# Decode attention block: wide Q chunks, paired PV matmuls, single score banks and a software pipeline one stage deeper

## The chip, the cores and the metric

The kernel runs on one core of one Trainium2 chip. The metric is the time of one execution on the device in microseconds (us); lower is better. The kernel before stands at 206.03 us, the median of 4 runs (204.81 to 207.11). Engines are named as in the profile: PE (matmul), PEld (weight load), DVE (vector), ACT (scalar), POOL, SP (issues DMAs).

## The reference, cut to what matters

A transformer block for one decode token and a batch of 2. Per batch and head (32 heads of 192), one query row meets the last 1024 rows of a K and a V cache; then come an output projection and a gated FFN. Layer norms are modulated by a projected condition `c`.

```python
mod = silu(c) @ w_mod                                  # 640 x 3840 weights
h = layernorm(x) * (1 + ca) + sa
q = (h @ wq).reshape(2, 1, 32, 192)                    # 640 x 6144
scores = einsum('bhqd,bhkd->bhqk', q, k[:, :, -1024:]) * 192 ** -0.5
o = einsum('bhqk,bhkd->bhqd', softmax(scores), v[:, :, -1024:])
x = x + ga * (o @ wo)                                  # 6144 x 640
h = layernorm(x) * (1 + cb) + sb
x = x + gb * ((gelu(h @ w_gate) * (h @ w_up)) @ w_down)
```

Every weight and every cache row is read once: 76.88 MB, all bf16.

## The kernel before

All large loads go through the SP queue in one order: the first third of `w_mod`, four parts of `wq`, the rest of `w_mod`, 64 cache items of 768 KB (K or V of one head, both batches) through a ring of 10 slots, then `wo`, `w_gate`, `w_up`, `w_down`. A "group" is two heads times two batches: four units, two K items and two V items. Scores are made on DVE and PE: DVE multiplies K by the broadcast query (`mul`), PE adds up 32-column chunks of the product in PSUM with identity matmuls (`red`), and DVE sums the last 32 columns (`D3`). Then comes the softmax chain: maximum over partitions by a transpose (`T`), its broadcast (`Bc`), `D7`, `exp`, then `PV`.

```python
BK_S = (0, 1, 2, 3)                       # score banks: two for even groups, two for odd
declare_q(QL - 1)                         # QL = NG: all 32 Q units, here, ahead of attention
mod_part(1)
...
for g in range(NG + 1):
    d_mul(g, 0); p_reduce(g, 0)
    chain_a1(g - 1)                       # D3 over 128x1024 f32, D4, T
    filler(g)                             # nothing left to do: QL = NG and ND = 0
    d_mul(g, 1); declare_ring([4 * g]); p_reduce(g, 1)
    chain_a2(g - 1)                       # D5, D6 (ACT), Bc (PE)
    d_mul(g, 2); p_reduce(g, 2)
    chain_a3(g - 1)                       # D7, exp (ACT)
    p_pv(g - 1)                           # 32 matmuls of 192 columns
    declare_ring([4 * (g - 1) + 2, 4 * (g - 1) + 3])   # V slots free: next loads
    filler(g)
    d_mul(g, 3); declare_ring([4 * g + 1]); p_reduce(g, 3)
    chain_b1(g - 1); chain_b2(g - 1)      # divide, select rows, transpose into oT
# (guards for the first and last g are cut)
```

Each engine runs its list in order; a scheduler puts in the semaphore waits from declared reads and writes.

## Time and profile before

| | before |
|---|---|
| span of the profiled run | 203.3 us |
| PE, DVE busy | 68%, 46% |
| load stream (queue 1) | 99.1% of 16 engines' time |
| first attention multiply | 45.6 us |
| a group when nothing makes it wait | 6.36 us |
| a group of loads (4 x 768 KB) | 7.8 us |

The page of the kernel before; the row of 40 slices is mean DMA busy share in tenths, below it GB/s; a group line has count, busy us, mean ns and idle time with its releaser; the last line gives KB and the median time from issue to landing.

```profile
PE 139.0 (68%) x1809; PEld 93.2 (46%) x1809; DVE 92.7 (46%) x176; ACT 45.8 (23%) x140; POOL 1.2 (1%) x9
...
DMA  5999999999999999999999999999999999999990
GB/s 171 407 402 401 401 413 411 400 401 401 401 342 413 399 399 400 401 402 399 402 402 401 399 402 399 403 400 401 402 400 403 386 363 363 362 369 398 394 332 28
...
q1 hardware_dynamic: 30468, 76.88, 99.1%
...
L423 PE MATMUL ps<-prod,ident_b 128*128 128x256 bf16 x384 | 63.1, 312 | 19.3 <-DVE prod L410 19.2
L410 DVE TENSOR_TENSOR prod<-ring,qbc 128x1536 bf16<-128x1536 bf16 x64 | 60.4, 948 | 8.8 <-DMA ring<-in_A_k_cache_dram 8.4
...
L370 PE MATMUL ps<-r 128*128 128x384 bf16 x160 | 27.7, 338 | 3.3 <-DVE r L351 3.3
...
L471 DVE TENSOR_REDUCE S_sb<-ps 128x32 f32<-128x1024 f32 x16 | 19.5, 1218 | 1.5 <-PE ps L423 1.5
...
ring<-in_A_k_cache_dram SPq DMA_DIRECT2D x32, 768.0 KB, 9.7
```

The load stream is the bottleneck: 9 in every slice but the first and last, and the multiplies (L410) idle for K loads. The stretch of 363 GB/s at slices 32 to 35 is `wo`, whose rows are 1280 B, as are those of `w_down` at the very end; everything else has rows of 2560 B and more and runs at about 400.

The chain of waits through one group at the one place where compute doesn't wait for loads (start us, us, what):

```profile
57.34 0.96 DVE prod L410
58.29 1.15 DVE S_sb L471
...
59.46 0.19 DVE M L475
59.65 0.88 DVE prod L410
...
60.57 0.83 PE ps L423 x6
61.40 0.31 PE ps L486 x2
61.71 0.76 PE ps L423 x6
62.47 0.76 PE ps L437 x31
...
63.32 0.28 ACT junk L448 x2
...
63.70 0.96 DVE prod L410
```

From multiply to multiply 6.36 us: this is what a group costs when its data is there. Loads need 7.8 us for the same group, so compute catches up with the loads and then waits for them.

One hole in the stream, by stretches of half a us (columns: busy time of PE, PEld, DVE, ACT, POOL, then PE clock, DMA share, GB/s):

```profile
58.00:58.50 0.50, 0.49 (x6) 0.37 (x7) 0.50 (x2) 0.12 (x1) 0.00 (x0) 1.00 0.81 184
58.50:59.00 0.50, 0.50 (x6) 0.36 (x4) 0.50 (x1) 0.05 (x1) 0.00 (x0) 1.00 0.79 160
```

The 32 Q units and the `mod` matmuls hold the first multiply back to 45.6 us, so no V slot comes free before 57 us and the stream dips.

### The profile page before, as it was taken

The numbers are of one execution on the slowest core, as the hardware profiler recorded it, in microseconds if no ns is written. First come the engines' busy times: TensorE is split into PE (matmuls) and PEld (weight loads), VectorE is DVE, ScalarE is ACT, GpSimd is POOL, SyncE is SP. The second block draws the span as 40 slices with busy tenths as digits, with TensorE's granted clock in tenths as the row PEclk, the third lists the DMA queues.
The fourth block names the chain that finished last, engine by engine and source line by source line (L and its number), as shares of the span: only waits on it lengthen the run. The fifth ranks groups of instructions, "written<-read, shape, count | busy, mean of one in ns | idle before, by whom it ended". The sixth has DMA issues, their size and how long they took to land.

```text
span 203.3 us, 4191 instructions
## 1 busy us (share of the span) xinstructions
PE 139.0 (68%) x1809; PEld 93.2 (46%) x1809; DVE 92.7 (46%) x176; ACT 45.8 (23%) x140; POOL 1.2 (1%) x9
## 2 busy tenths in 40 slices
PE   0339999978768774975976876849758766434343
PEld 0315555556445552643544544526525435434342
DVE  0050000008877786595586595675765840001300
ACT  2124566520322211111122121112112123000300
POOL 2000000000000000000000000000000000000000
PEclk9999999985999999698599699797978785555555
DMA  5999999999999999999999999999999999999990
GB/s 171 407 402 401 401 413 411 400 401 401 401 342 413 399 399 400 401 402 399 402 402 401 399 402 399 403 400 401 402 400 403 386 363 363 362 369 398 394 332 28
DMA packets 30526, 77.15 MB, mean 379 GB/s; under 512 B 1324, under 2 KB 9004, under 8 KB 30508
## 3 DMA queue, kind: packets, MB, share of 16 engines
q1 hardware_dynamic: 30468, 76.88, 99.1%
q8 instruction: 14, 0.23, 0.5%
q14 instruction: 4, 0.03, 0.0%
q10 hardware_dynamic: 40, 0.01, 0.0%
HBM read 76.88 MB, written 0.00 MB: 378 GB/s over the span
## 4 chain that ended last, share of the span: by engine, by line
PE 33%; DMA 26%; SPq 20%; DVE 16%; ACT 2%; issue 1%
SPq L247 20%; DMA ring<-in_A_k_cache_dram 17%; PE ps L370 14%; PE ps L423 10%; DVE prod L410 8%; DMA r<-in_B_w_down_dram 5%; DVE S_sb L471 5%; PE ps L437 4%; DMA r<-in_w_mod_dram 4%; PE ps L338 2%; PE ps L486 2%; DVE M L475 1%; ACT L494 1%; ACT junk L448 1%; DVE r L351 0%
## 5 line engine op out<-in xcount | busy, mean ns | idle before, releaser
L423 PE MATMUL ps<-prod,ident_b 128*128 128x256 bf16 x384 | 63.1, 312 | 19.3 <-DVE prod L410 19.2
L410 DVE TENSOR_TENSOR prod<-ring,qbc 128x1536 bf16<-128x1536 bf16 x64 | 60.4, 948 | 8.8 <-DMA ring<-in_A_k_cache_dram 8.4
L423 PEld LDWEIGHTS ps<-prod,ident_b 128*128 128x128 bf16 x384 | 36.8, 109 | 32.2 <-DVE prod L410 23.1
L370 PE MATMUL ps<-r 128*128 128x384 bf16 x160 | 27.7, 338 | 3.3 <-DVE r L351 3.3
L370 PEld LDWEIGHTS ps<-r 128*128 128x128 bf16 x160 | 15.2, 100 | 15.5 <-ACT qbc L374 3.6
L471 DVE TENSOR_REDUCE S_sb<-ps 128x32 f32<-128x1024 f32 x16 | 19.5, 1218 | 1.5 <-PE ps L423 1.5
L374 ACT ACTIVATE qbc<-ps 128x384 bf16<-128x384 f32 x32 | 15.7, 491 | 14.6 <-PE ps L370 14.6
L484 ACT ACTIVATE diag<-ident_f,gmn 4x4 f32<-4x4 f32 x16 | 4.7, 296 | 49.7 <-DVE gmn L482 49.7
L437 PE MATMUL ps<-ring,E_sb 128*1 128x192 bf16 x512 | 15.2, 267 | 0.7 <-ACT E_sb L494 0.7
L396 DVE TENSOR_SCALAR opc<-modT 128x10 f32<-128x10 f32 x1 | 0.2, 173 | 31.3 <-ACT modT L343 31.3
L437 PEld LDWEIGHTS ps<-ring,E_sb 128*1 128x1 bf16 x512 | 10.6, 89 | 5.4 <-ACT E_sb L494 3.0
L551 PE MATMUL ps<-oT,r 128*128 128x2 bf16 x240 | 7.0, 165 | 8.4 <-DMA r<-in_A_wo_dram 8.4
L450 DVE RECIPROCAL rden<-den 128x1 f32<-128x1 f32 x16 | 2.6, 164 | 19.0 <-ACT junk L448 19.0
L551 PEld LDWEIGHTS ps<-oT,r 128*128 128x128 bf16 x240 | 6.7, 104 | 8.6 <-DMA r<-in_A_wo_dram 8.6
L477 PE MATMUL ps<-ident_f,M 128*4 128x128 f32 x16 | 4.6, 290 | 8.0 <-DVE M L475 7.9
L486 PEld LDWEIGHTS ps<-diag,ones_f 4*128 4x128 f32 x32 | 5.9, 229 | 5.4 <-issue 4.5
L448 ACT ACTIVATE junk<-ps 128x8 f32<-128x8 f32 x16 | 2.8, 178 | 22.6 <-PE ps L440 22.6
L494 ACT ACTIVATE E_sb<-Sb_sb 128x32 bf16<-128x32 f32 x16 | 3.7, 229 | 18.9 <-DVE Sb_sb L491 18.9
L486 PE MATMUL ps<-diag,ones_f 4*128 4x4 f32 x32 | 7.3, 296 | 0.7 <-ACT diag L484 0.7
L452 ACT ACTIVATE On<-ps,rden 128x192 bf16<-128x192 f32 x16 | 6.7, 421 | 3.9 <-DVE rden L450 3.9
L557 DVE TENSOR_TENSOR lnt<-ps,modT 128x10 f32<-128x10 f32 x1 | 0.2, 170 | 16.3 <-PE ps L551 16.3
L477 PEld LDWEIGHTS ps<-ident_f,M 128*4 128x4 f32 x16 | 1.3, 81 | 12.6 <-DVE M L475 12.6
(66 smaller groups left out, 76.8 us busy)
## 6 DMA issues: line engine op xcount, KB each, us to landing
ring<-in_A_k_cache_dram SPq DMA_DIRECT2D x32, 768.0 KB, 9.7
ring<-in_A_v_cache_dram SPq DMA_DIRECT2D x32, 768.0 KB, 12.4
r<-in_A_wq_dram SPq DMA_DIRECT2D x4, 1920.0 KB, 18.0
r<-in_A_wo_dram SPq DMA_DIRECT2D x4, 1920.0 KB, 18.7
r<-in_w_mod_dram SPq DMA_DIRECT2D x1, 3200.0 KB, 25.1
r<-in_B_w_gate_dram SPq DMA_DIRECT2D x1, 1920.0 KB, 17.4
r<-in_B_w_up_dram SPq DMA_DIRECT2D x1, 1920.0 KB, 17.0
r<-in_w_mod_dram SPq DMA_DIRECT2D x1, 1600.0 KB, 7.1
```

Of the source, the lines that this page charges most:

```text
L247: return lambda e: e.dma_start(dst, src)
L370: last = e.matmul(ps[:, bk, 0:QN], lhsT=hbc_v[:, k, b, :], rhs=wq_v[:, k, g * QN:(g + 1) * QN], start=(k == 0), stop=(k == KT - 1))
L374: S.op("act", (lambda g, b, bk: lambda e: e.activation(out=qbc[:, 2 * g:2 * g + 2, b, :], in_=ps[:, bk, 0:QN].rearrange("p (h d) -> p h d" ...
L410: return S.op("dve", lambda e: e.tensor_tensor(out=prod[:, pslot, :, :], in0=ring[:, ks, b, :, :], in1=qbc[:, h, b:b + 1, :].broadcast_to( ...
L423: last = e.matmul(o_ap, lhsT=ident_b[:, :], rhs=prod[:, pslot, :, ci * GC:(ci + 1) * GC], start=(ci == 0), stop=(ci == NCH - 1))
L437: e.matmul(ps[32 * i:32 * i + 1, BK_O, 0:Dh], lhsT=E_sb[:, z, i, j:j + 1], rhs=ring[:, vs, b, j, :], start=(j == 0), stop=(j == J - 1), ti ...
L452: S.op("act", lambda e: e.activation(out=On[:, z, :], in_=ps[:, BK_O, 0:Dh], func=ACTF.Identity, scale=rden[:, z:z + 1]), reads=[bank(BK_O ...
L471: S.op("dve", lambda e: e.tensor_reduce(out=S_sb[:, z, :, :], in_=ps[:, b0:b0 + NBG, 0:UPB * J * GC].rearrange("p k (u j c) -> p (k u) j c ...
L477: S.op("pe", lambda e: e.transpose(ps[0:4, BK_T, 0:P], M1[:, z, :], ident_f[:, :]), reads=[("M1", z), "ident_f"], writes=[bank(BK_T)], nam ...
L486: S.op("pe", lambda e: e.matmul(ps[:, BK_T, P:P + 4], lhsT=ones_f[0:4, :], rhs=diag[:, z, :], start=True, stop=True), reads=[("diag", z), ...
L494: S.op("act", lambda e: e.activation(out=E_sb[:, z, :, :], in_=Sb_sb[:, z, :, :], func=ACTF.Exp, scale=SCALE), reads=[("Sb", z)], writes=[ ...
L551: last = e.matmul(ps[:, BK_M, 2 * jn:2 * jn + 2], lhsT=wo_v[:, t, jn * P:(jn + 1) * P], rhs=oT[:, t, :], start=(t == 0 and jn == 0), stop= ...
```

## The change

Its intent, as the code shows: Q in chunks of 512 columns (24 units in place of 32 of 384), only 6 of them ahead of attention and two more per group as "filler"; after they run out, warm matmuls in the filler places to keep the PE clock up; score chunks of 64 columns (3 reduce matmuls of 512 in place of 6 of 256), which fill all four score banks with one group; PV on two key rows at a time (16 matmuls of 384 columns in place of 32 of 192); division and selection pushed one group later.

```diff
-    GC = 32
+    GC = 512 // J                        # 64: NCH = 3
-    QL = NG
-    ND = 0
+    QW = 512
+    QUP = min(2 * NQC, 2 * ((3 * 2 * Dh + QW - 1) // QW))   # 6 units ahead
+    ND = 4                               # warm matmuls per filler, 128x512
...
-        S.dma("act", ... cr ...); S.dma("act", ... xr ...)
+        S.dma("sp", ... cr ...); S.dma("sp", ... xr ...)     # ahead of w_mod
...
-            bk = BK_S[NBG * (g % 2) + i // UPB]
+            bk = BK_S[i]                 # all four banks belong to one group
...
-  in_=ps[:, b0:b0 + NBG, 0:UPB * J * GC]   # D3: 1024 elements
+  in_=ps[:, 0:4, 0:J * GC]                 # D3: 2048 elements
...
-                for j in range(J):        # PV: lhsT 128x1, rhs 128x192
+                for jp in range(J // 2):  # PV: lhsT 128x2, rhs 128x384
...
-        for g in range(NG + 1):
+        for g in range(NG + 2):
             d_mul(g, 0)
-            p_reduce(g, 0)
+            chain_b2(g - 2)
             chain_a1(g - 1)
-            filler(g)
+            p_reduce(g, 0)
+            chain_b3(g - 2)
             d_mul(g, 1); declare_ring([4 * g]); p_reduce(g, 1)
             chain_a2(g - 1)
+            filler()                      # Q unit or warm, between Bc and PV
             d_mul(g, 2); p_reduce(g, 2)
             chain_a3(g - 1); p_pv(g - 1)
             declare_ring([4 * (g - 1) + 2, 4 * (g - 1) + 3])
-            filler(g)
+            chain_b1(g - 1)
             d_mul(g, 3); declare_ring([4 * g + 1]); p_reduce(g, 3)
-            chain_b1(g - 1); chain_b2(g - 1)
+            filler()
```

(Guards, renamings and the selection matmuls of `chain_b3`, now 8 in place of 4, are cut.)

## The prediction

> **What bounds the kernel now.** The DMA engines. In the slice table the DMA row is 9 from slice 1 to 37, about 400 GB/s (363 near 162-180 us), while PE is busy 68% and DVE 46% (busy table). 76.88 MB pass in a 203.3 us span. By the landing events one K or V item (768 KB) lands every 1.95 us, so a group of four takes 7.8 us. A group's compute, where the timeline shows it not waiting for data (52 to 70 us), takes 6.4 us; later the first multiply waits for its K (idle put down to the K load, 8.4 us in all). The chain of waits ends in queued weight loads from 147 us and the last w_down landing at 200.1 us.
>
> One hole: the windows at 57.5-59.5 us show 160-330 GB/s. All 32 Q units run first (PE L370, 13.96 to 41.7 us), then the mod matmuls, so the first multiply starts at 45.65 us though its K landed about 38 us; the ring's next loads wait for PV until 57 us. That is about 0.8 us of transfer. But the landing events, 16 per load, show that the slowest DMA engine kept its 1.95 us pace through it; only leading engines idled (spread of landings fell from 1.9 to 1.2 us). The end waits for the slowest.
>
> **What the change does.**
> - Bytes, and the order of the large loads: unchanged.
> - Q: 160 matmuls of 384 become 120 of 512: same columns, but only 30 matmuls stand before attention. First multiply near 40 us. The hole goes.
> - Reduce: 384 matmuls of 256 become 192 of 512. PV: 512 of 192 become 256 of 384. Same columns, fewer instructions, little PE time.
> - D3 reads 2048 instead of 1024 elements: 1.22 us becomes about 2.3 (estimate: twice, less a fixed part). DVE per group 5.8 to 6.9 us busy, a group about 7.4: below 7.8, closer. Score banks are no longer doubled, so a group's first reduce waits for D3.
> - PV comes some 2 us later after K's landing; the ring then still has about 10 us of loads queued: no starvation. Warm matmuls: off the path.
> - The c and x loads move from the ACT queue to the head of SP. Their issues took 0.63 and 0.29 us; the w_mod load, issued at 0.81 us, and all behind it start about 0.7 us later (estimate). The Trainium skill, "DMA: Bandwidth & Descriptors", section "Issuing engines are not separate DMA queues", says a second issuing engine saves just this.
> - Instruction fetches: 14 of 16 KB in the DMA queue table, about 1.08 us each; some steps of the slowest engine's lag (0.8 to 3 us over the run) follow them. The Trainium skill, "Runtime: NRT & Kernel Launch", section "Instruction fetch mechanics", gives 256 instructions a block; 3618 PE instructions agree with 14. After: about 2900, so 11; worth about -0.5 us (estimate).
>
> **Sum.** +0.7 start, -0.5 fetches, -0.1 hole: within noise. 206.1 us, range 204.4 to 207.6. The runs before scatter from 204.8 to 207.1.
>
> **Signs.** First multiply near 40 us; no dip near 57 us; DMA share still over 97%; D3 about 2.3 us; first w_mod issue about 1.5 us; 11 fetches; last w_down landing 199.5-201; the 3.2 us tail unchanged.
>
> **What would make it wrong.** A group above 7.8 us on DVE or a cold PE (clock 0.5) for all 16 groups, draining the queue: slower by several us. Or the hole, the early multiply or fewer fetches speeding the slowest engine more than I see: at most 2-3 us.

## The result, and the profile after

| | before | after |
|---|---|---|
| median of all runs | 206.64 us (16 runs) | 212.09 us (11 runs) |
| ratio of fast runs | | 1.0259, 95% interval 1.0216 to 1.0301 |
| span of the profiled run | 203.3 us | 209.5 us |
| first attention multiply | 45.6 us | 39.6 us |
| group, start of D3 to next start of D3 | 7.8 us mostly | 8.40 us with Q units, 7.95 with warm matmuls, 9.5 twice |
| D3, mean | 1.22 us | 2.29 us |
| PE instruction fetches (16 KB) | 14 | 11 |

The ratio is the mean time of one kernel's fast runs over that of the other's of the same rounds, so it is not quite the ratio of the medians; three runs of the changed kernel over 213 us count as slow and are left out of it. The change is slower by 2.6%, although its first multiply comes 6 us earlier.

The page of the changed kernel, with the clock row as well (tenths of full PE clock granted):

```profile
PE 135.8 (65%) x1424; PEld 68.6 (33%) x1441; DVE 110.6 (53%) x176; ACT 43.6 (21%) x132; POOL 1.2 (1%) x9
...
PEclk9999965569999999999999999997998799555555
...
GB/s 128 410 399 403 403 413 409 400 402 402 400 385 372 411 356 377 388 364 409 341 358 412 312 372 381 378 404 399 360 415 353 386 370 364 363 364 396 395 339 25
...
q1 hardware_dynamic: 30508, 76.89, 97.5%
...
L396 DVE TENSOR_TENSOR prod<-ring,qbc 128x1536 bf16<-128x1536 bf16 x64 | 59.5, 947 | 6.0 <-DMA ring<-in_A_k_cache_dram 6.0
L408 PE MATMUL ps<-prod,ident_b 128*128 128x512 bf16 x192 | 54.1, 394 | 1.8 <-DVE prod L396 1.8
L415 DVE TENSOR_REDUCE S_sb<-ps 128x32 f32<-128x2048 f32 x16 | 36.7, 2291 | 3.7 <-PE ps L408 3.7
...
L373 PE MATMUL ps<-qbc,ident_b 128*128 128x512 bf16 x49 | 14.5, 418 | 0.4
...
ring<-in_A_k_cache_dram SPq DMA_DIRECT2D x32, 768.0 KB, 6.7
```

The stream is no longer steady: GB/s falls to 312 to 390 in most slices of attention, and queue 1 is busy 97.5% in place of 99.1%. The multiplies do about the same work; D3 (L415) has grown from 19.5 to 36.7 us and warm matmuls (L373) are new. K loads now land 6.7 us after issue in place of 9.7: there is less queued ahead of them. PE's clock is better than before (0.869 of full on average in the profiled run, against 0.827), so it is not what made the change slower.

The chain of waits through one group of the changed kernel:

```profile
82.65 2.30 DVE S_sb L415
...
84.98 0.20 DVE M L419
...
85.22 0.27 PE ps L421
85.49 0.65 PE ps L408 x3
...
86.46 0.67 PE ps L408 x3
87.13 0.31 PE ps L430 x2
87.44 1.20 PE ps L359 x5
...
88.66 0.60 ACT qbc L363
89.26 0.13 ACT E_sb L438
...
89.43 0.82 PE ps L450 x15
...
90.26 0.77 PE ps L408 x3
...
91.05 2.30 DVE S_sb L415
```

From D3 to D3, 8.40 us, and not one step of it is a load. The loop runs: D3 2.30, D4 0.20, transpose 0.27, first reduce 0.65, selection (in the cut lines) 0.3, second reduce 0.67, broadcast 0.31, **Q unit on PE 1.20, its eviction on ACT 0.60**, exp 0.13 (the rest of it hidden), PV 0.82, last reduce 0.77, and D3 again. Seven groups in a row have this length. With warm matmuls in the filler's place 0.97 us of them stand in the chain, and the group is 7.95 us:

```profile
121.02 0.97 PE ps L373 x4
```

Both lengths are over the 7.8 us of the loads. The wait list of the SP queue (us in total, times, longest) shows the loads waiting for PV. Before:

```profile
SPq L93 <- PE ps L440: 69.4, 13, 7.4
```

and after:

```profile
SPq L93 <- PE ps L454: 81.2, 13, 8.8
```

The landing records (16 for each load, one per DMA engine) add it up: from the last landing of the first cache item to that of the 64th, 125.0 us pass before and 131.1 us after. That is 6.1 us, about all of the difference of the two spans (6.2 us).

### The profile page after: what moved, and what is told of

It is laid out like the page before. It is cut to its first block, busy times and chain, and to the rows that moved or that the text cites. A ratio compares the mean times of both kernels' runs of the same rounds, so it can differ in the third digit from the quotient of the medians.

```text
span 209.5 us, 3411 instructions
## 1 busy us (share of the span) xinstructions
PE 135.8 (65%) x1424; PEld 68.6 (33%) x1441; DVE 110.6 (53%) x176; ACT 43.6 (21%) x132; POOL 1.2 (1%) x9
## 3 DMA queue, kind: packets, MB, share of 16 engines
q1 hardware_dynamic: 30508, 76.89, 97.5%
## 4 chain that ended last, share of the span: by engine, by line
PE 33%; SPq 32%; DVE 16%; DMA 13%; ACT 4%; issue 2%
SPq L242 32%; PE ps L408 14%; DVE S_sb L415 14%; DMA ring<-in_A_k_cache_dram 8%; DMA r<-in_B_w_down_dram 5%; PE ps L450 5%; PE ps L359 5%; PE ps L373 3%; ACT qbc L363 2%; PE ps L430 2%; PE ps L421 2%; PE ps L477 1%; DVE M L419 1%; ACT L438 1%; ACT E_sb L438 1%
## 5 line engine op out<-in xcount | busy, mean ns | idle before, releaser
L408 PE MATMUL ps<-prod,ident_b 128*128 128x512 bf16 x192 | 54.1, 394 | 1.8 <-DVE prod L396 1.8
L415 DVE TENSOR_REDUCE S_sb<-ps 128x32 f32<-128x2048 f32 x16 | 36.7, 2291 | 3.7 <-PE ps L408 3.7
L359 PE MATMUL ps<-r 128*128 128x512 bf16 x110 | 29.3, 405 | 4.3 <-DVE r L341 3.7
L363 ACT ACTIVATE qbc<-ps 128x512 bf16<-128x512 f32 x24 | 14.3, 597 | 42.4 <-PE ps L359 42.4
L408 PEld LDWEIGHTS ps<-prod,ident_b 128*128 128x128 bf16 x192 | 16.8, 100 | 18.8 <-issue 5.0
L450 PE MATMUL ps<-ring,E_sb 128*2 128x384 bf16 x256 | 13.8, 336 | 3.2 <-ACT E_sb L438 3.2
L373 PE MATMUL ps<-qbc,ident_b 128*128 128x512 bf16 x49 | 14.5, 418 | 0.4
L469 ACT ACTIVATE On<-ps,rden 128x384 bf16<-128x384 f32 x16 | 9.3, 579 | 1.8 <-DVE rden L467 1.8
L450 PEld LDWEIGHTS ps<-ring,E_sb 128*2 128x2 bf16 x256 | 4.7, 82 | 12.6 <-ACT E_sb L438 7.3
L477 PE MATMUL ps<-sel,On 128*128 128x2 bf16 (+1 forms) x64 | 7.4, 183 | 1.2 <-ACT On L469 1.2
```

The lines of the kernel that those rows point to most:

```text
L359: last = e.matmul(ps[:, bk, 0:w], lhsT=hbc_v[:, k, b, :], rhs=wq_v[:, k, c0:c0 + w], start=(k == 0), stop=(k == KT - 1))
L363: S.op("act", lambda e: e.activation(out=qbc[:, b, c0:c0 + w], in_=ps[:, bk, 0:w], func=ACTF.Copy), reads=[bank(bk)], writes=[("qbc", cq, ...
L373: last = e.matmul(ps[:, BK_Q[0], 0:QW], lhsT=ident_b[:, :], rhs=qbc[:, 0, 0:QW], start=True, stop=True)
L408: last = e.matmul(o_ap, lhsT=ident_b[:, :], rhs=prod[:, pslot, :, ci * GC:(ci + 1) * GC], start=(ci == 0), stop=(ci == NCH - 1))
L415: S.op("dve", lambda e: e.tensor_reduce(out=S_sb[:, z, :, :], in_=ps[:, 0:4, 0:J * GC].rearrange("p k (j c) -> p k j c", j=J), axis=AX.X, ...
L450: e.matmul(ps[32 * i:32 * i + 2, BK_O, 0:ON], lhsT=E_sb[:, z, i, 2 * jp:2 * jp + 2], rhs=ring[:, vs, b, 2 * jp:2 * jp + 2, :], start=(jp = ...
```

## The experiments

Theory A: the group is set by a serial loop through DVE, PE and ACT, and the change lengthened it past the pace of the loads with three things at once: the doubled D3, a first reduce that must wait for it, and a filler placed between broadcast and PV. Rival B: it is D3 alone, as DVE work. Rival C: the loads themselves got slower, by the later start or by contention. All runs below computed correct results. Times are medians; ratios are to the kernel before on the same chip. The group lengths are from start to start of D3 in each trace.

### e1_filler_late: the filler out of the loop

```diff
             chain_a2(g - 1)
-            filler()
             d_mul(g, 2); p_reduce(g, 2)
             ...
             p_reduce(g, 3)
+            filler()
             filler()
```

> Edit: the filler (Q unit or warm matmuls) that stood between the broadcast matmul and the PV matmuls is moved behind the last reduce of the group, where DVE runs the 2.3 us score reduction anyway. Theory A (a serial loop through PE, ACT and DVE sets the group: 8.39 us with a Q unit in it, 7.95 with warm matmuls, against 7.82 us of DMA): about 1.4 us leave the loop, free-running group about 7.0 us, so the group falls back to the DMA pace of 7.8; time 205 to 207 us, no dips in GB/s during attention, share of DMA on queue 1 back to about 99%. Rival B (the doubled score reduction on DVE by itself sets the group, the filler is innocent): group stays near 8.4, 211 to 213 us. Rival C (DMA itself got slower, by the move of c and x or by contention): no change either.

Measured: 205.35 us (205.04 to 205.42), ratio 0.9941 (0.9899 to 0.9982). Its groups are 7.8 to 7.9 us throughout, the last one, which waits for nothing, 7.07. The page's GB/s row, and D3 in its list of groups:

```profile
GB/s 122 409 401 402 401 415 409 401 400 402 402 399 402 401 400 402 401 402 399 402 399 401 402 401 402 400 403 401 402 399 402 386 363 364 363 366 401 390 313 13
...
L415 DVE TENSOR_REDUCE S_sb<-ps 128x32 f32<-128x2048 f32 x16 | 36.4, 2274 | 0.2 <-PE ps L408 0.2
```

The dips are gone: the stream runs at about 400 GB/s through all of attention. D3 is still 2.27 us here, so rival B is out, and no load was touched, so rival C is out. The PE work of the filler is the same; it now runs while DVE does D3.

### e2_score_banks: only the score banks as before

```diff
-    GC = 512 // J
+    GC = 32                               # UPB = 2, NBG = 2
-            bk = BK_S[i]
+            bk = BK_S[NBG * (g % 2) + i // UPB]
-  in_=ps[:, 0:4, 0:J * GC]
+  in_=ps[:, b0:b0 + NBG, 0:UPB * J * GC]
```

> Edit: only the score banks as before (32-column chunks, two banks per group in turn, D3 over 1024 elements, 24 reduce matmuls of 256); fillers and everything else as after. Theory A: the loop loses about 1.07 us of D3, 8.39 becomes about 7.3 with a Q unit and 6.9 with warm matmuls, both below 7.82: time 205 to 207 us. If only the filler's place mattered and D3 were off the loop, it would stay at 211 to 213. Rival C: no change.

Measured: 205.47 us (205.24 to 205.56), ratio 0.9948 (0.9907 to 0.9990). D3 is 1.21 us; the one early group that waits for no load takes 7.35 us and the last 6.9, as the sum said. The chain through that early group:

```profile
56.14 1.24 DVE S_sb L420
...
57.91 0.66 PE ps L412 x6
...
63.49 1.24 DVE S_sb L420
```

So the filler's place was not "the" cause either: D3's growth or the filler, taken out alone, brings the loop under the pace of the loads. They are causes only together. The third term, the first reduce behind D3, is still in this chain (the 0.66 us at 57.91, because PE's list puts it after the transpose); no run takes it out alone, so its share is read from the chain and not shown by an experiment.

### e3_no_warm: the change without warm matmuls

```diff
-    ND = 4
+    ND = 0
```

> Edit: warm matmuls taken away (count 0), Q units stay where they are. Theory A: only the last six or so groups change, from 7.95 (9.5 when the clock is down) to about 7.0 free-running, so DMA-paced; they catch up about 1 to 3 us: 209 to 211 us. If the warm matmuls were off the path, as the prediction said: 212 us, no change. If they earned their keep by holding the clock up: slower than 212.

Measured: 211.34 us (209.28 to 211.78), ratio 1.0208 (1.0149 to 1.0267). The range given just misses it. The last seven groups are 7.09, 7.09, 7.67, 9.38, 9.55, 9.90 and 8.51 us: 59.2 in sum, against 58.8 in the change. The loop did shrink to the 7.1 us foreseen, and then the clock fell and gave it back. Warm matmuls are on the path *and* hold the clock; here the two about cancel.

### e4_cx_act: c and x loaded from ACT again

```diff
-        S.dma("sp", k_dma(cr[:, :], ...)); S.dma("sp", k_dma(xr[:, :], ...))
+        S.dma("act", k_dma(cr[:, :], ...)); S.dma("act", k_dma(xr[:, :], ...))
```

> Edit: the c and x loads issued from ACT as before, the rest as after. Theory A: the first weight load is issued about 0.8 us earlier, but attention is bound by the loop, and the first K for group 1 comes 0.4 us earlier: minus 0.0 to 0.5 us, 211.5 to 212. Rival C (the start of the stream costs the 5 us): back to 206 or 207.

Measured: 212.05 us, ratio 1.0260 (1.0205 to 1.0314). Rival C's 206 or 207 is out. No difference shows, but the interval reaches 1 us to either side, so a cost of some tenths could hide in it: that the later start is free while the loop sets the time fits this run and isn't shown by it.

### e5_warm_double: eight warm matmuls in place of four

```diff
-    ND = 4
+    ND = 8
```

> Edit: the change with its warm matmuls doubled, 8 in place of 4 at each filler place. Theory A (the filler between broadcast and PV lies in the loop): each of the last seven or so groups grows by the 0.97 us that four warm matmuls take, 7.95 to about 8.9 us; the filler behind the last reduce stays hidden behind the 2.3 us score reduction; time 216 to 219 us. If warm matmuls are off the path: 212 us.

Measured: 214.05 us (212.94 to 215.59), ratio 1.0388 (1.0321 to 1.0455). The direction and the group are as foreseen: 8.81 to 8.82 us in all of the last seven groups. The time fell short of the range because I had forgotten that two of the change's last seven groups ran at 9.5 us on a lowered clock, and with doubled warm matmuls the profiled run has no such group: 61.7 us for the seven against 58.8, 2.9 more; the medians differ by 2.0.

### b1_q_spread and b3_q_mostly_early: the early start alone, in the kernel before

```diff
-    QL = NG
+    QL = 4                                # b1_q_spread; QL = 12 in b3_q_mostly_early
```

> Edit: the kernel before, with only the first 8 of its 32 Q units ahead of attention; the other 24 go to its own filler places, two in each group. The hole in the transfers near 57 us should go and the first multiply come at about 40 us, as in the change. Theory A: its group is about 6.4 us plus one Q unit of 0.9 us in the loop, about 7.2 to 7.8, not over the 7.82 us of DMA, so it stays DMA-paced; and the slowest DMA engine gains little from the hole: 205 to 206.5 us, 0 to 0.7% faster. If an early start alone were worth what the hole shows (0.8 us) plus the 6 us of earlier multiply: 200 us. If Q units among the groups cost by themselves: 209 or more.

> Edit: the kernel before with 24 of its 32 Q units ahead of attention (8 in b1_q_spread), the last 8 in the first four groups. PE should end these 24 units about when the second w_mod load lands, so the first multiply comes near 40 us as in b1 and there is no hole near 57 us; but from the fifth group on there is no Q unit to keep the clock up. b1 was 0.8% faster than the kernel before (204.67 against 206.34) and scattered less. If that came from the early start and the closed hole: 204.6 to 205.0 here too. If it came from Q units holding the clock through more groups: 205.5 to 207 with the scatter of the kernel before. The prediction had put the hole at 0.1 us.

Measured: b1 204.67 us (204.59 to 204.87), ratio 0.9924 (0.9888 to 0.9960); b3 204.79 us (204.52 to 205.10), ratio 0.9933 (0.9884 to 0.9981). Both start attention near 39 to 40 us. In b3 the groups from the fifth on have no Q unit and its mean clock is that of the kernel before (0.827), yet it gains as much. So the gain comes with the early start, not with the clock. It is 1.2 to 1.7 us in the medians, where I had written 0.1 for the hole. Both also scatter far less than the kernel before (205.2 to 207.8 in the same rounds). Which part of that the hole itself makes isn't shown: the one profiled run of before was one of its fast ones (205.07 us), and its span is only 0.3 us over that of b3.

### e6_late_act: e1 and c and x from ACT

The edit is that of e1 with that of e4.

> Edit: e1_filler_late and in addition the c and x loads from ACT as before. Now that the DMA stream bounds the kernel again, the start of the stream should count one for one: first weight load issued at about 0.8 instead of 1.6 us, first w_mod landing 0.4 to 0.8 us earlier; 204.6 to 205.0 us against 205.35 of e1_filler_late. In the loop-bound change the same edit gave nothing (212.05 against 212.09).

Measured: 204.76 us (204.43 to 205.01), ratio 0.9926 (0.9889 to 0.9962), on another chip than e1. The same edit that showed nothing in the loop-bound change gives about 0.6 us here; in the traces the last `w_down` landing comes at 199.82 us in place of 200.36.

### e7_late_act_wide and e9_wide_wo: longer rows for the late weights

With the loop short, the end is the end of the load stream, and 9.8 MB of it move in 1280 B rows at 363 GB/s. Both versions, built on e6, deal attention features to partitions so that a partition reads three neighbouring rows of `wo`; e7 does the same with the rows of `w_down`, which needs strided columns of `w_gate` and `w_up`.

```diff
-  A_wo[...].rearrange("(t p) n -> p t n", p=P)             # 1280 B rows
+  A_wo[...].rearrange("(g p t) n -> p g (t n)", p=P, t=3)  # 3840 B rows
   # selection: columns t, t+3, t+6, ... of On go to tile t
+  On3 = On[:, z, :].rearrange("p (r d t) -> p r t d", r=2, t=3)
+  for t in range(3):
+      for hh in range(2):
+          two(ps[64 * hh:64 * hh + 64, BK_O, OTC + 2 * t:OTC + 2 * t + 2], t, 2 * hh, ...)
   # e7 only
-  lhsT=wv[:, k, fc * P:(fc + 1) * P]
+  lhsT=wv[:, k, :].rearrange("p (m f) -> p f m", f=FC)[:, fc, :]
-  B_w_down[f0 * P:(f0 + nf) * P, :].rearrange("(f p) n -> p f n", p=P)
+  B_w_down.rearrange("(p f) n -> p f n", p=P)[:, f0:f0 + nf, :]
```

> Edit: e6_late_act and in addition wo and w_down loaded with longer rows: features are dealt to partitions so that each partition reads 3 neighbouring rows of wo (3840 B in place of 1280 B) and all its rows of a w_down part (7680, 5120, 2560 B in place of 1280 B); the selection matmuls and the gate and up matmuls take strided columns to match. 9.8 MB now move at about 363 GB/s; at the 402 GB/s of the 3 KB rows that is 2.6 us less. Theory A (DMA stream bounds the end once the loop is short): 201.8 to 202.8 us, below both kernels. If row length doesn't set that rate: as e6.

Measured: 202.67 us (202.45 to 202.81), ratio 0.9825 (0.9789 to 0.9861). The stream did get shorter, with 404 to 410 GB/s where 363 stood, but PE took over the end. The gate and up matmuls of e7, from the list of groups:

```profile
L566 PE MATMUL ps<-h2T,r 128*128 128x2 bf16 x120 | 7.4, 198 | 3.3 <-DVE h2T L317 2.4 <-DMA r<-in_B_w_up_dram 0.9
```

and of e9, which keeps their columns contiguous:

```profile
L566 PE MATMUL ps<-h2T,r 128*128 128x2 bf16 x120 | 3.5, 165 | 5.0 <-DMA r<-in_B_w_up_dram 2.5 <-DVE h2T L317 2.4
```

Only the order of columns differs, and PE's busy time goes from 3.5 to 7.4 us.

> Edit: e7_late_act_wide with w_down and the gate and up matmuls as before, so only wo is loaded with 3840 B rows. In e7 the strided gate and up weight loads took 3.6 us for 60 in place of 1.7, and put PE (not the last landing) at the end of the chain: up weights landed at 192.4 us, matmuls to 198.2. Expected: the four wo loads still take about 4.9 us each in place of 5.4; w_down again about 5.1 us; last w_down landing about 197.5 us in the trace, and the end 3.2 us later: 202.2 to 202.7 us, 0 to 0.4 less than e7.

Measured: 202.34 us (202.24 to 202.46), ratio 0.9813 (0.9786 to 0.9841). Here the last chain is the last landing again (`w_down`, 197.31 us in the trace).

### e10_wide_no_warm: e9 without warm matmuls

```diff
-    ND = 4
+    ND = 0
```

> Edit: e9_wide_wo with the warm matmuls taken away. With fillers out of the loop and the group paced by DMA, theory A says that warm matmuls buy nothing: same as e9 within 0.3 us, with a lower granted clock in attention. If the clock that they hold matters even here, groups run over 7.82 us in the last third and the time goes up by 1 us or more.

Measured: 206.22 us (204.99 to 209.53), ratio 0.9976 (0.9928 to 1.0024): 3.9 us over e9 in the medians. My expectation was wrong, its alternative right. These runs scatter widely: three of the six are at 205.0 to 205.4 us, and the profiled one, at 208.0, is the second longest, so its trace shows more than the usual loss. Its first nine intervals are 7.8 to 7.9 us, as in e9; once Q units run out they are 10.0 to 10.2. PE on the timeline where that begins (start, us; in brackets the idle time before and who ended it):

```profile
120.23 0.27 PE L421 MATMUL ps<-ident_f,M 128*4 128x128 f32 x1 [3.24 <-DVE M L419]
```

PE stood idle for 3.24 us, until D4 had followed D3. One of the groups after it (columns as above, the clock after POOL):

```profile
138.03:148.16 10.13, 7.52 (x47) 2.55 (x47) 6.49 (x10) 1.43 (x6) 0.00 (x0) 0.66 0.83 311
```

and the same stage of e9, with warm matmuls:

```profile
142.00:150.00 8.00, 6.50 (x56) 2.74 (x55) 6.40 (x10) 1.43 (x6) 0.00 (x0) 1.00 1.03 400
```

The clock is 0.66 on average in place of 1.00, the reduce and PV steps of the chain grow from 0.65 to 0.8 us each to about 1.4 (the first reduce stays at 0.75 to 0.86), and the loop that takes 7.1 us at full clock takes 10.1: over the pace of the loads again.

The clock's own records suggest why it doesn't come back. From 120.81 to 172 us it is half for 6.83 us and full for 3.41, in turn, 10.24 us together, about the length of the slow group. So the full stretch keeps falling on the wait for D3, with little PE work in it, and a half stretch follows each time. That one leads to the other is a reading of these records, not tested:

```profile
127.64:131.05 3.41, 0.81 (x5) 0.30 (x4) 3.17 (x3) 0.00 (x0) 0.00 (x0) 1.00 1.03 373
131.05:137.88 6.83, 6.83 (x45) 2.26 (x43) 3.32 (x7) 1.43 (x6) 0.00 (x0) 0.50 0.87 341
```

Nor does a drop need an idle gap of 3 us. In the kernel before, a half stretch follows one in which PE worked 1.48 of 3.41 us and was never idle for more than 1.43 us:

```profile
78.46:81.87 3.41, 1.48 (x11) 0.94 (x12) 3.38 (x6) 0.22 (x1) 0.00 (x0) 1.00 1.03 398
81.87:85.28 3.41, 3.41 (x37) 2.16 (x38) 1.67 (x3) 0.31 (x2) 0.00 (x0) 0.50 1.04 404
```

Warm matmuls do earn their keep, when they stand where PE would idle for D3.

### b2_spread_wide_wo: the kernel before with two small edits

The edit is that of b1 with the `wo` rows of e9.

> Edit: b1_q_spread (the kernel before with 8 Q units ahead of attention) and in addition wo in 3840 B rows. If the end of every DMA-paced version is the end of the weight stream, the gain adds up as it does in the change's pipeline: 204.67 less about 2.1, that is 202.3 to 202.8 us, level with e9. Then wide Q chunks, paired PV and the deeper pipeline bring nothing that this kernel can use.

Measured: 202.25 us (202.08 to 202.41), ratio 0.9809 (0.9781 to 0.9836), level with e9. It has no warm matmuls; its slowest groups are 8.55 us, two of them near the end. Q spread out and wide `wo` rows in the old pipeline give all that the best form of the new pipeline gives. Both are faster than either kernel of the comparison.

## Why the prediction was wrong

I predicted 206.1 us, 204.4 to 207.6, a difference within noise; measured is 212.09. Several signs came true all the same: first multiply 39.6 us, D3 2.29, first `w_mod` issue 1.61, 11 fetches, and a DMA share of 97.5%, which was asked to stay over 97% and so was too loose to show the starved stream. The last `w_down` landing, expected at 199.5 to 201 us, came at 206.2.

- **The load stream bounds the kernel before: right.** Every version whose loop is under 7.8 us lands at 202 to 207 us, and follows the stream in its start (e6) and in its row length (e9).
- **"DVE per group 5.8 to 6.9 us busy, a group about 7.4: below 7.8": this step failed.** DVE is busy 6.49 us per group as foreseen, and D3 2.29. But I took the free group before (6.36), added what D3 grew by (1.07), and stopped. The group is a loop over three in-order engines, and two more terms went into it: the filler between broadcast and PV (1.80 us with a Q unit and its eviction, 0.97 with warm matmuls), and a first reduce that no longer runs ahead of D3 (0.65, and selection 0.3, now after it; the prediction says that this reduce waits for D3, and gives the wait no time); in return the two multiplies of the old chain (0.96 and 0.88) are hidden. 6.36 + 1.07 + 1.80 + 0.95 - 1.84 is 8.3; measured is 8.40. This counts the main terms only: with warm matmuls it gives 7.5, where 7.95 is measured, because a third reduce (0.65) that the eviction used to hide then stands in the chain. A step that is not the busiest engine's work was counted as free.
- **"Warm matmuls: off the path": wrong as the change places them** (e5: 0.87 us per group for four more), true behind the last reduce (e1). And they are not idle ornament: e10 loses 3.9 us without them.
- **"The ring then still has about 10 us of loads queued: no starvation": wrong.** I read the 10 us off the kernel before, whose compute was faster than its loads and kept the ring full of requests. By the landing records, when the change issued its 13th cache load at 56.8 us, the loads before it had only 3.9 us left to land. The kernel before had no more at that load (3.1 us), but its shorter loop built that up to between 4.5 and 8.0 us at the first K load of each later group. In the change 2.2 to 3.3 us were left there while the Q units lasted, and the stream moved 365 to 394 GB/s in these groups in place of about 400; e1, with the filler out of the loop, holds 6.3 to 6.4. A queue lends its depth once; a loop that is too long by 0.6 us asks for it in every group.
- **Start, +0.7 us:** the issue moved as foreseen (0.81 to 1.61 us). It costs about 0.6 us where the stream counts (e1 against e6, on two chips) and nothing that the runs can tell in the change (e4).
- **Hole, -0.1 us: probably too small.** b1 and b3 gain 1.2 to 1.7 us with an early start in the kernel before, though how much of it is the hole's isn't shown. My argument from the slowest DMA engine holds in the profiled run, and that run was one of the fast ones.
- **Fetches, -0.5 us: not seen.** The count went to 11 as foreseen; no run changes it alone, but b1 with 14 fetches (204.67) and e6 with 11 (204.76) are level, and so are e1 with 11 and e2 with 13.
- **What would make it wrong:** "a group above 7.8 us on DVE" named the right threshold and the wrong engine: it was no single engine.

What stays open: what makes the kernel before scatter over 3 us when b1 and b3 scatter over less than 0.6; and why b2's groups without warm matmuls stop at 8.55 us where e10's go to 10.1 and stay. The shorter D3, during which PE idles, is a likely reason, argued and not shown; it fits that e10's PE is idle for 2.60 us in each slow group and b2's, in all of attention, only once for more than 1.0 us (2.31 us, up to 142.3 us).

## What to carry to other kernels

Before moving work "off the critical path", write down the loop that a pipelined group makes through all in-order engines, from one instance of a step to its next, and compare its sum, not the busiest engine's, with the pace of the loads. Put filler work where its own engine waits for another one, never between a result and the step that frees a buffer; the same warm matmuls cost about 0.9 us per group in one place (7.95 us against 7.09 without them in e3) and saved 3.9 us in all in another (e9 against e10). A full request queue in the profile is evidence that compute is ahead now, not a reserve that a slower loop can spend in every iteration.

## What the Trainium skill lacked or had wrong

- "DMA: Bandwidth & Descriptors", section "Specifications", gives 512 B as the least transfer for line rate. Here rows of 1280 B ran at 363 GB/s and rows of 3840 B at 403 to 410 in the same place of the same stream (e6 against e9); that was worth about 2.4 us of 205.
- "TensorE: Matmul & The Clock Gate", section "What's actually happening", has the clock fall after an idle window of about 3.4 us and rise after one of sustained work. The length agrees: e10's clock changes after 3.41 us or multiples of it. A wholly idle window isn't needed: the kernel before fell to half after 3.41 us with 1.48 us of PE work and no idle gap over 1.43 us. Nor was one there in e10's slow groups, where the clock stayed at 0.66 on average with idle gaps of 2.60 us.
- "TensorE: Matmul & The Clock Gate", section "Weight-path perf modes — Fast Weight Load (FWL) and DoubleRow", has the fast load on for 128 weights that aren't FP32, and doesn't say what a step between their columns costs. Bf16 weights with a column step of 24 B took 7.4 us for 120 matmuls against 3.5 us with contiguous columns (e7 against e9). Whether the fast load was off or was fed slowly isn't shown.
- "Runtime: NRT & Kernel Launch", section "Instruction fetch mechanics": the block size agrees (14 fetches for 3618 PE instructions); that fetches are mostly hidden fits too, against my charge of 0.5 us for three of them (b1 with 14 fetches and e6 with 11 are level), though no run here changes the count alone.
